# Diagonal score blocks half computed and half mirrored through memory, and a reordered start of the experts

## The chip, the cores and the metric

The kernel runs on one core of one Trainium2 chip. The metric is device time in microseconds (us) of one execution. The median of three runs is 1388.75 us (1388.1 to 1389.97). TensorE multiplies matrices (PE in the profile, with its weight loads as PEld), VectorE is DVE, ScalarE is ACT, GpSimd is POOL, and SyncE (SP) issues most of the DMA transfers, one after the other.

## The reference

For each of 8 batches, with `u`, `v` of 2496 x 256 and `z` of 2496 x 64, all in 32-bit floats:

```python
scores = (1 / S) * z @ z.T
attn   = maximum(scores, 0) ** 2
x      = u * (attn @ v)
```

All 19968 rows of `x` then go to a mixture of 8 experts: a gate `x @ w_gate` picks one expert for each row, each expert keeps the 80 rows with the highest gate weight, and writes `gate * (maximum(x @ w1, 0) @ w2)` for them. Every other row of the output is zero.

## The kernel before

**Tiles.** A batch's 2496 rows are 20 tiles of 128 keys (the last one holds its 64 rows twice, with `v` arranged so that they add up once), taken as 10 pairs. The queries are cut into 5 chunks, `qc` 0 to 4, of 512 columns each; chunk 4 has 448. The main loop has 8 x 5 x 10 = 400 steps `(b, qc, r)`; step `r` handles one pair of key tiles, in the order of `pairs_of[qc]`: 0 to 9, and in chunk 3 first 8 and 9.

**A step.** `scores` runs two steps ahead of its use (LOOK = 2). For each of the pair's two tiles TensorE makes a 128 x 512 block of scores with two matmuls (L326, L327), ScalarE applies Relu (L330) and Square (L331), and the square is split into a rounded high part `ah` and a rest `al` (L105 or L107, and L54). `attend` then adds the pair into two accumulators with twelve matmuls (L358 to L360), the three products of high and low parts for each tile and each half of `v`'s columns.

**Mirrored blocks.** Scores are symmetric. A 512 x 512 block above the diagonal is computed once; VectorE transposes its 32 x 32 squares (L265), SP writes them to memory (`y`, L275) and reads them back with the squares in their mirrored places (`blk`, L292), and `mirrored` only splits the block into `ah` and `al` (L310, L54). SP works through its transfers in program order and waits before the read until the write has landed. Blocks on the diagonal are computed whole: pairs `2*qc` and `2*qc+1`.

**Around it.** While a chunk runs, `finished` treats the chunk before it at fixed steps `r`: `x` is split for the gate, stored transposed (`chunk_store`, L427, and `chunk_store2`), its logits are made, and after a batch the gate's sums and the counts of rows for each expert follow. The next batch's `z` and `v` are loaded and split at fixed steps too. The order on TensorE, ScalarE, VectorE and SP is that of the program text. In the last two chunks of the last batch the first experts' weights are split (`weights_ahead`, L624 and L625).

**After the loop.** The last three key tiles of the last chunk are attended one half of the columns at a time, `x` is formed (`chunk_x_last`, L377), the logits give the last rows' expert (L416 and the operations of `gate_top`), the counts and running sums `incl` give each expert's 80 places, and `ranks` says which running numbers these are.

**The experts** (`ahead`, unit i is expert i). A place is found in three moves: `block` compares its rank with the running sums of blocks of 256 rows, a table row of that block (`wtab`) gives the row inside it, and `token` makes the row number and has GpSimd gather the row of `x` (`xg`, L1104). For units 0 and 1 the table row comes from a TensorE product (`pe_table`, `pe_block`, `pe_fetch`), for the others by a gather from memory (`fetch`, L1046). `whole` reassembles the row, `ffn_x` transposes it, `ffn1` and `ffn2` are the two layers with split weights (L1166, L1196), `result` scales and scatters. `split` rounds one loaded quarter of an expert's weights on ScalarE and takes the rest on VectorE. In this part TensorE, ScalarE, VectorE and GpSimd follow the text, and SP is ordered by the framework.

Of the kernel before, what the change touches and what calls it, by code (L numbers as in the profile page):

```python
# [25 lines left out]
def attn_moe_kernel(ctx, tc, zT, uT, v, wg, w1, w2, out, seq, cap):  # L26
# [172 lines left out]
    def constants():  # L199
        nc.gpsimd.memset(ones_b, 1.0)  # L200
        nc.gpsimd.memset(gall, 0.0)
        for e in range(E):
            nc.gpsimd.memset(first_w[:, :, e:e + 1], float(E - e))
# [24 lines left out]
    tot = const.tile([P, E, NBLK], F32, name="tot")  # L228
    incl = const.tile([P, E, NBLK], F32, name="incl")
    rank = const.tile([P, NST, E], F32, name="rank")  # L230
    ex_last = const.tile([P, NT, E], F32, name="ex_last")
# [14 lines left out]
    pairs_of = [list(range(NP)) for qc in range(NQ)]  # L246
    pairs_of[NQ - 2] = [NP - 2, NP - 1, *range(NP - 2)]
# [9 lines left out]
    to_read = [(b, i, j, (b * NQ + i) * NP + pairs_of[i].index(2 * j) - LOOK)  # L257
# [37 lines left out]

    def pair_tile(tag, b, qc, k, dt=F32R, bufs=3):
        return ew.tile([P, 2, CH], dt, tag=tag, name=f"{tag}_{b}_{qc}_{k}", bufs=bufs)
# [17 lines left out]
    def scores(b, qc, k):  # L315
# [4 lines left out]
        zc, zd = zc_t[b, qc], zd_t[b, qc]  # L320
        a = pair_tile("a", b, qc, k, F32, 2)
        ss = []
        for h in range(2):
            zk = zc_t[b, k // QT][:, (k % QT + h) * P:(k % QT + h + 1) * P]
            s = ps_s.tile([P, CH], F32, tag="s", name=f"s_{b}_{qc}_{k + h}")
            nc.tensor.matmul(s[:, :nq], zk, zc[:, :nq], start=True, stop=False)  # L326
            nc.tensor.matmul(s[:, :nq], zk, zd[:, :nq], start=False, stop=True)  # L327
            ss.append(s)
        for h, s in enumerate(ss):
            nc.scalar.activation(out=a[:, h, :nq], in_=s[:, :nq], func=AF.Relu)  # L330
        nc.scalar.activation(out=a[:, :, :nq], in_=a[:, :, :nq], func=AF.Square)  # L331
        ah = pair_tile("ah", b, qc, k)
        on_v = k // QT == qc or (qc, k) in ON_V and b > 0
        cp(V if on_v else nc.scalar, ah[:, :, :nq], a[:, :, :nq])
        al = pair_tile("al", b, qc, k)
        tt(al[:, :, :nq], a[:, :, :nq], ah[:, :, :nq], ALU.subtract)
# [7 lines left out]
    def attend(b, qc, k, cols=range(DC)):  # L344
        nq = min(CH, seq - qc * CH)
        first, last = 2 * pairs_of[qc][0], 2 * pairs_of[qc][-1] + 1
# [117 lines left out]
    def gate_top(b, q0, q1):  # L464
# [17 lines left out]
        ex = ex_last[:, q0 * QT:q1 * QT] if last else small("ex")  # L482
# [27 lines left out]
    def gate_sum(b, ex, pool):  # L510
# [7 lines left out]
        tt(s4, ex[:, :, 0::2], ex[:, :, 1::2], ALU.add)  # L518
        s2 = small("s2", E // 4)
        tt(s2, s4[:, :, 0::2], s4[:, :, 1::2], ALU.add)  # L520
        s1 = small("s1", 1)
        tt(s1, s2[:, :, 0:1], s2[:, :, 1:2], ALU.add)
        ts(s1, s1, 1e-9, ALU.add)
        V.reciprocal(out=gall[:, col:col + NT], in_=s1.rearrange("p t o -> p (t o)"))
# [8 lines left out]
    def count(k0, k1):  # L533
# [5 lines left out]
        nc.scalar.copy(out=tot[:, :, k0:k1], in_=tp[:, :n].rearrange("p (k e) -> p e k", e=E))  # L539
# [146 lines left out]
    WARM = 3, 6  # L686
    WARM0 = 8
    steps = [(b, qc, r) for b in range(B) for qc in range(NQ) for r in range(NP)]
# [32 lines left out]
    def finished(b, qc, r):  # L721
# [14 lines left out]
        if r == (5 if at_end else 6):  # L736
# [3 lines left out]
        if b < B - 1 and qc == NQ - 1:  # L740
            if r == 7:
                gate_top(b, 0, NQ)
            elif r == 8:
                gate_sum(b, gate_near(b, 0), gp)
        elif qc == 0 and b > 0:
            part = kb - BPB, kb
            if r == 2:
                count(*part)
            elif r == 4:
                up_to(*part)  # L750
                blocks(ps_m, "m", gp, oh, *part)
        elif at_end:
# [12 lines left out]
    with tc.manual_schedule(engines={ET.PE, ET.Activation, ET.DVE, ET.SP}):  # L765
# [11 lines left out]
        for i, (b, qc, r) in enumerate(steps):  # L777
# [4 lines left out]
            if i + LOOK < len(steps):  # L782
                nb, nqc, nr = steps[i + LOOK]
                scores(nb, nqc, 2 * pairs_of[nqc][nr])
# [10 lines left out]
            p = pairs_of[qc][r]  # L795
# [9 lines left out]
            if b + 1 < B:  # L805
                if r == 1:
                    z_raw[b + 1, qc] = load_z(b + 1, qc)
                if r == 5:
                    prep_zc(b + 1, qc, z_raw.pop((b + 1, qc)))
# [3 lines left out]
                if qc == NQ - 1:  # L813
                    g = (r - 1) // 2 if r < 9 else 4
                    if r in (2, 4, 6, 8, 9):
# [12 lines left out]
            mirror_out()  # L828
            if r == NP - 1:
# [183 lines left out]
    def steps_of(own, tl, tw, ps_t, ps_h):  # L1013
        sl, xg_t, tk_t, xs_t, x_t, h_t, hT_t, o_t = {}, {}, {}, {}, {}, {}, {}, {}
# [13 lines left out]

        def block(i):

            st, e = units[i]
            le = tw.tile([P, 1 + NBLK], F32, tag="le", name=f"le_{i}{own}")
            if i < 2:
                nc.gpsimd.memset(le[:, 0:1], 1.0)
# [57 lines left out]
        def token(i):  # L1092
# [16 lines left out]
            tk_t[i] = tok, j, base  # L1109

        def place(i):
# [6 lines left out]
            tk_t[i] = tok, slo  # L1118

        def fetch_gate(i):  # L1120

            ns, (tok, slo) = num(i), tk_t[i]
# [4 lines left out]
            tk_t[i] = gg, slo  # L1127
# [27 lines left out]
        def ffn1(i, part):  # L1155
# [8 lines left out]
            for c in range(DC):  # L1164
                for x, w in ((xh, w1h), (xl, w1h), (xh, w1l)):
                    nc.tensor.matmul(hp[:ns], x[:, c * ns:(c + 1) * ns], w[:, c, f0:f0 + 512],  # L1166
                                     start=n == 0, stop=n == 3 * DC - 1)
                    n += 1
# [242 lines left out]
```

## Time and profile before

| What | Value |
|---|---|
| median of 3 runs | 1388.75 us |
| the profiled execution's own time | 1388.46 us |
| its span, first to last instruction | 1386.6 us |
| TensorE's mean granted clock | 0.992 |
| main loop, first to last attention matmul | about 10 to 1305 us |

The page divides the span into busy time of each engine, and the views used below ask the same trace more closely: a table of stretches, groups of instructions by line, lists of waits, and the timeline. A bracket in a timeline row gives the idle time of the engine just before, and what ended it. The ends of matmuls are modelled, so the distance between two starts says more than a duration.

### The profile page before, as it was taken

To read this page: it belongs to the slowest core of one execution; us is meant where nothing else is said; L and a number is where in the kernel's file an instruction comes from. 1 tells how busy PE (TensorE), PEld (TensorE's weight loads), DVE (VectorE), ACT (ScalarE), POOL (GpSimd) and SP (SyncE) were. 2 spreads that over 40 slices of the span, in tenths; PEclk is the share of its full clock that TensorE was granted. 3 is DMA by queue.
4 is the path that set the end of the run, shared out by engine and by line. 5 is a ranking of instruction groups with operands and counts; after the bars stand their busy time and mean duration, and the time that the engine had idled before them with its cause. 6 is when DMAs were issued, how large, how long until landed. Compare 5 with 4: busy or idle time off the path is not lost. (4 is left out here: it accounts for less than half of the span.)

```text
span 1386.6 us, 19562 instructions
## 1 busy us (share of the span) xinstructions
PE 1367.1 (99%) x7087; PEld 1139.5 (82%) x7087; DVE 1060.6 (76%) x1517; ACT 1008.8 (73%) x1282; POOL 36.5 (3%) x57
## 2 busy tenths in 40 slices
PE   9999999999999999999999999999999999999887
PEld 6888888888888888888888888888888888888666
DVE  8876788668877788767886688777787678867785
ACT  8866687758777587666887577775877668876375
POOL 0000000000000000000000000000000000000062
PEclk9999999999999999999999999999999999999989
DMA  6899877995888958997688958889588986789774
GB/s 223 252 249 271 225 204 239 235 267 143 256 237 231 273 151 245 239 261 197 188 252 232 270 143 259 238 225 274 145 246 239 255 210 179 220 229 252 176 225 141
DMA packets 260070, 311.89 MB, mean 225 GB/s; under 512 B 96152, under 2 KB 188192, under 8 KB 249728
## 3 DMA queue, kind: packets, MB, share of 16 engines
q1 hardware_dynamic: 258752, 309.02, 81.4%
q0 software_dynamic: 1216, 1.56, 0.4%
q8 instruction: 57, 0.93, 0.3%
q14 instruction: 45, 0.37, 0.1%
HBM read 153.48 MB, written 126.37 MB: 202 GB/s over the span
## 5 line engine op out<-in xcount | busy, mean ns | idle before, releaser
L359 PE MATMUL acc<-ah,vt 128*128 128x512 f32 (+1 forms) x1520 | 584.5, 385 | 0.3 <-DVE vt L146 0.3
L360 PE MATMUL acc<-al,vt 128*128 128x512 f32 (+1 forms) x1520 | 584.5, 385 | 0.3 <-DVE al L54 0.2
L358 PE MATMUL acc<-ah,vt 128*128 128x512 f32 (+1 forms) x1520 | 584.2, 384 | 0.0
L54 DVE TENSOR_TENSOR al<-a,ah 128x1024 fp32r<-128x1024 f32 (+1 forms) x240 | 291.5, 1214 | 135.4 <-ACT ah L105 125.6
L330 ACT ACTIVATE a<-s 128x512 f32<-128x512 f32 (+1 forms) x480 | 258.4, 590 | 153.9 <-PE s L327 143.8
L359 PEld LDWEIGHTS acc<-ah,vt 128*128 128x128 f32 x1520 | 285.4, 188 | 53.9 <-DVE vt L146 1.2
L358 PEld LDWEIGHTS acc<-ah,vt 128*128 128x128 f32 x1520 | 285.3, 188 | 52.9
L360 PEld LDWEIGHTS acc<-al,vt 128*128 128x128 f32 x1520 | 285.4, 188 | 52.9 <-DVE al L54 1.2
L331 ACT ACTIVATE a<-a 128x1024 f32<-128x1024 f32 (+1 forms) x240 | 253.0, 1054 | 7.6
L310 ACT CAST ah<-blk 128x1024 fp32r<-128x1024 f32 x160 | 167.0, 1049 | 105.6 <-PE acc L359 88.5
L54 DVE TENSOR_TENSOR al<-blk,ah 128x1024 fp32r<-128x1024 f32 x160 | 193.8, 1216 | 56.1 <-ACT ah L310 53.2
L265 DVE STREAM_TRANSPOSE x<-a 128x512 f32<-128x512 f32 x320 | 207.6, 687 | 0.0
L327 PE MATMUL s<-zd,zc 128*128 128x512 f32 (+1 forms) x480 | 186.5, 388 | 0.0
L105 ACT CAST ah<-a 128x1024 fp32r<-128x1024 f32 x153 | 160.9, 1052 | 4.8
L107 DVE CAST ah<-a 128x1024 fp32r<-128x1024 f32 (+1 forms) x87 | 59.2, 681 | 95.6 <-ACT a L331 95.6
L326 PE MATMUL s<-zc,zc 128*128 128x512 f32 x320 | 128.1, 400 | 0.0
L327 PEld LDWEIGHTS s<-zd,zc 128*128 128x128 f32 x480 | 90.3, 188 | 16.3 <-issue 0.5
L326 PEld LDWEIGHTS s<-zc,zc 128*128 128x128 f32 x320 | 60.1, 188 | 11.1
L326 PE MATMUL s<-zc 128*128 128x512 f32 (+1 forms) x160 | 63.5, 397 | 0.0
L388 ACT CAST xb<-xf 128x1024 bf16<-128x1024 f32 (+1 forms) x39 | 40.0, 1026 | 23.4 <-DVE xf L377 23.1
L396 ACT CAST xb<-xr 128x1024 bf16<-128x1024 f32 (+1 forms) x39 | 39.9, 1024 | 15.5 <-DVE xr L54 15.5
L377 DVE SCALAR_TENSOR_TENSOR xf<-acc,ut 128x512 f32<-128x512 f32 (+2 forms) x82 | 50.1, 653 | 0.0
(171 smaller groups left out, 835.9 us busy)
## 6 DMA issues: line engine op xcount, KB each, us to landing
y<-x SPq DMA_DIRECT2D x80, 1024.0 KB
blk<-y SPq DMA_DIRECT2D x320, 256.0 KB
out<-idle SPq DMA_DIRECT2D x40, 512.0 KB
vraw<-v SPq DMA_DIRECT2D x32, 512.0 KB
ut<-uT SPq DMA_DIRECT2D x32, 512.0 KB
xs<-xq SPq DMA_DIRECT2D x32, 512.0 KB
wraw<-w SPq DMA_DIRECT2D x28, 512.0 KB
zd<-zc SPq DMA_DIRECT2D x78, 128.0 KB
```

What stands on the lines that cost most here:

```text
L54: V.tensor_tensor(out=o, in0=a, in1=b, op=op)
L105: eng.copy(out=o, in_=i)
L107: eng.tensor_copy(out=o, in_=i)
L265: V.transpose(out=x[:, :, :, t].rearrange("p n k s -> p k n s"), in_=a)
L310: nc.scalar.copy(out=natural(ah), in_=src)
L326: nc.tensor.matmul(s[:, :nq], zk, zc[:, :nq], start=True, stop=False)
L327: nc.tensor.matmul(s[:, :nq], zk, zd[:, :nq], start=False, stop=True)
L330: nc.scalar.activation(out=a[:, h, :nq], in_=s[:, :nq], func=AF.Relu)
L331: nc.scalar.activation(out=a[:, :, :nq], in_=a[:, :, :nq], func=AF.Square)
L358: nc.tensor.matmul(o, vt[:, t, 0, cs], ah, start=k == first, stop=False)
L359: nc.tensor.matmul(o, vt[:, t, 1, cs], ah, start=False, stop=False)
L360: nc.tensor.matmul(o, vt[:, t, 0, cs], al, start=False, stop=k == last)
```

## The change

- Diagonal blocks are no longer computed whole, but for three (`whole_block`: the first of all, and the last two chunks of the last batch). The upper pair `2*qc` is computed over all 512 columns (in chunk 4 too) and comes first in the chunk's order; VectorE transposes its right half (`quarter_out`), SP writes 256 KB and reads it back (`quarter_write` at r = 0, `quarter_back` at r = 3, into one buffer). The lower pair `2*qc+1` comes last; its scores are computed from column 256 on, and the left 256 columns are split from the copy in memory.
- To make room, the next batch's `z` and `v` are prepared at other steps, and the finished chunk's store, logits and sums come some steps later.
- The running sums of the last batch's first 18 half tiles are made by one scan after the last attention, instead of eight additions inside the loop; `tot` is kept in 16 bits.
- The last sums of the gate are made by GpSimd, ahead of the experts, and the gate's comparison `gate_near` of the last chunk is put right behind `gate_top`. Three warming matmuls follow the last logits.
- In the experts, units 2 and 3 get their table rows from TensorE too, the rows for units 4 and 5 are gathered before unit 0 begins, the second half of expert 2's weights is loaded at once, `ffn1` does the products of `xl` last, and the weight splits are spread 1, 3, 4, 4, 4, 4, 4 over the units instead of 3, 4, 3, 3, 4, 3, 3, 1.

```diff
+    def whole_block(b, qc):
+        return (b, qc) in ((0, 0), (B - 1, NQ - 2), (B - 1, NQ - 1))
+    def order(b, qc):
+        rest = [p for p in range(NP) if p // 2 != qc]
+        if whole_block(b, qc):
+            return [NP - 2, NP - 1, *range(NP - 2)] if qc == NQ - 2 else list(range(NP))
+        if qc == NQ - 2:
+            rest = rest[-2:] + rest[:-2]
+        return [2 * qc, *rest, 2 * qc + 1]
...
+    def quarter_out(b, qc, a):
+        x = zpool.tile([P, n32, 2, 2, SQ], F32, tag="md", name=f"xd_{b}_{qc}", bufs=1)
+        for t in range(2):
+            V.transpose(out=x[:, :, :, t].rearrange("p n k s -> p k n s"), in_=a[:, t, HQ:])
+        quarter[b, qc] = now[0], x
+    def quarter_write():
+        for (b, qc), (at, x) in list(quarter.items()):
+            if at is not None and at + 2 <= now[0]:
+                y = dram.tile([n32, SQ, n32, 4 * SQ], F32, tag="yd", name=f"yd_{b}_{qc}", bufs=2)
+                nc.sync.dma_start(out=y.rearrange("g p h f -> (g p) (h f)"),
+                                  in_=x.rearrange("p h k t s -> p (h k t s)"))
+                quarter[b, qc] = None, y
+    def quarter_back(b, qc):
+        _, y = quarter.pop((b, qc))
+        m = zpool.tile([P, n32, 2, 2 * SQ], F32, tag="md", name=f"md_{b}_{qc}", bufs=1)
+        for h in range(n32):
+            nc.sync.dma_start(out=m[h * SQ:(h + 1) * SQ].rearrange("p g k f -> p g (k f)"),
+                              in_=y[:, :, h].rearrange("g p f -> p g f"))
+        quarter[b, qc] = None, m
...
+        diag = k // QT == qc and not whole_block(b, qc)
+        lower = diag and k % QT > 0
+        c0, c1 = (HQ, nq) if lower else (0, CH if diag else nq)
...
+            nc.tensor.matmul(s[:, c0:c1], zk, zc[:, c0:c1], start=True, stop=False)
+            nc.tensor.matmul(s[:, c0:c1], zk, zd[:, c0:c1], start=False, stop=True)
...
+        if lower:
+            m = quarter.pop((b, qc))[1].rearrange("p n k (t s) -> p k t n s", t=2)
+            nc.scalar.copy(out=natural(ah), in_=m)
+            tt(natural(al), m, natural(ah), ALU.subtract)
...
+        eng.tensor_tensor(out=s4, in0=ex[:, :, 0::2], in1=ex[:, :, 1::2], op=ALU.add)
+        eng.tensor_tensor(out=s2, in0=s4[:, :, 0::2], in1=s4[:, :, 1::2], op=ALU.add)
+        eng.tensor_tensor(out=s1, in0=s2[:, :, 0:1], in1=s2[:, :, 1:2], op=ALU.add)
+        eng.tensor_scalar(out=s1, in0=s1, scalar1=1e-9, scalar2=None, op0=ALU.add)
...
+        V.tensor_tensor_scan(out=sums.rearrange(fl), data0=keep.rearrange(fl),
+                             data1=pre["count"].rearrange(fl), initial=0.0,
+                             op0=ALU.mult, op1=ALU.add)
+        tt(incl[:, :, k0:k1], sums, incl[:, :, k0 - 1:k0].broadcast_to([P, E, n]), ALU.add)
...
-    SPLITS = dict(zip([(qb, 0), (qb, 2), (qb, 5), (qb, 8), (qz, 2), (qz, 4), (qz, 6), (qz, 8)], early))
+    SPLITS = dict(zip([(qb, 0), (qb, 2), (qb, 5), (qb, 8), (qz, 2), (qz, 4), (qz, 6), (qz, 7)], early))
+    keys_in = {qc: [(qc - 1, 1, 6)] for qc in range(1, NQ)}
+    keys_in[0] = []
+    keys_in[NQ - 1] = [(NQ - 2, 1, 4), (NQ - 1, 4, 7)]
...
-        if r == (3 if at_end else 1):
+        if r == (3 if at_end else 4):
             chunk_store(b, qc)
-        if r == (5 if at_end else 3):
+        if r == (5 if at_end else 6):
             chunk_store2(b, qc)
-        if r == (5 if at_end else 6):
+        if r == (5 if at_end else 6 if qc == NQ - 1 else 7):
             chunk_logits(b, qc)
...
-                count(*part)
-                up_to(*part)
-                half()
+                count(*part, True)
...
+            if b and qc == 0 and r == 3:
+                prep_v(b, NQ - 1, v_raw.pop((b, NQ - 1)), nc.scalar, V)
...
+            quarter_write()
+            if r == 3 and not whole_block(b, qc):
+                quarter_back(b, qc)
...
+        up_to_last((B - 1) * BPB, B * BPB - 2)
+        half()
         chunk_store(*prev)
         chunk_logits_last(*prev)
+        warm(3, ps_s, "s")
         gate_top(b, NQ - 1, NQ)
+        gate_near(b, NQ - 1)
+        gate_rows(b, ex_last, gp, nc.gpsimd)
...
             tot_last(NBLK - 2, NBLK)
+            raw_whole(*RAW[None])
+            pe_fetch(0)
+            warm_up(3)
+            for i in range(2, 4):
+                pe_table(i)
+            within(0)
+            token(0)
+            pe_fetch(1)
+            warm_up(4)
+            within(1)
+            last_gates()
+            token(1)
+            for i in range(2, 4):
+                block(i)
+                pe_block(i)
+            warm_up(2)
+            block(4)
+            fetch(4)
+            whole(0)
+            block(5)
+            fetch(5)
+            ffn_x(0)
+            for i in range(2, 4):
                 pe_fetch(i)
+            ffn_xl(0)
+            within(2)
+            token(2)
             ready.extend(kept)
             loads(2, PL)
             whole(1)
             within(3)
             token(3)
...
```

## Rows read from the trace of the kernel before

**Rows 1.** The page's part 1: busy us (share of span) xinstructions of each engine.

```profile
PE 1367.1 (99%) x7087; PEld 1139.5 (82%) x7087; DVE 1060.6 (76%) x1517; ACT 1008.8 (73%) x1282; POOL 36.5 (3%) x57
```

**Rows 2.** Stretches: busy us of PE, PEld, DVE, ACT, POOL; PEclk, DMA share, GB/s.

```profile
333.90:368.60 34.70, 34.70 (x176) 28.66 (x175) 29.13 (x43) 28.63 (x38) 0.00 (x0) 1.00 0.63 179
368.60:402.90 34.30, 34.30 (x177) 28.07 (x176) 29.22 (x52) 27.44 (x37) 0.00 (x0) 1.00 0.86 248
...
437.60:466.90 29.30, 29.30 (x152) 24.19 (x151) 20.27 (x22) 15.29 (x18) 0.00 (x0) 1.00 0.99 270
...
333.90:495.90 162.00, 162.00 (x837) 136.01 (x836) 124.57 (x168) 119.35 (x150) 0.00 (x0) 1.00 0.84 227
```

**Rows 3.** Timeline of PE in chunks 0 and 4 of batch 2: start us, us, matmul.

```profile
340.22 0.39 PE L326 MATMUL s<-zc,zc 128*128 128x512 f32 x1
...
343.84 0.39 PE L326 MATMUL s<-zc,zc 128*128 128x512 f32 x1
...
471.74 0.36 PE L358 MATMUL acc<-ah,vt 128*128 128x448 f32 x1
...
476.81 0.36 PE L359 MATMUL acc<-ah,vt 128*128 128x448 f32 x1
```

**Rows 4.** Timeline of PE, one unit of the experts: matmuls of 256 columns.

```profile
1336.48 0.80 PE L1181 MATMUL tp<-ident,h 80*128 80x80 f32 x8
...
1340.05 0.28 PE L1196 MATMUL op<-w2h,hTh 128*80 128x256 f32 x1
...
1342.74 0.28 PE L1196 MATMUL op<-w2h,hTl 128*80 128x256 f32 x1
1342.86 0.72 PE L1181 MATMUL tp<-ident,h 80*128 80x80 f32 x8
```

**Rows 5.** Groups by line: xcount | busy us, mean ns of one | idle us before <-releaser.

```profile
L358 PEld LDWEIGHTS acc<-ah,vt 128*128 128x128 f32 x1520 | 285.3, 188 | 52.9
...
L265 DVE STREAM_TRANSPOSE x<-a 128x512 f32<-128x512 f32 x320 | 207.6, 687 | 0.0
...
L54 DVE TENSOR_TENSOR s<-ex_last 128x80 f32<-128x80 f32 x1 | 0.2, 243 | 0.0
```

**Rows 6.** The same view, VectorE alone, from 1300 us to the end.

```profile
L625 DVE TENSOR_TENSOR w2l<-wraw,w2h 128x1024 fp32r<-128x1024 f32 x11 | 13.3, 1223 | 3.8 <-ACT w2h L624 3.7
...
L54 DVE TENSOR_TENSOR hTl<-tp,hTh 128x320 fp32r<-128x320 f32 x16 | 7.1, 483 | 2.0 <-ACT hTh L1185 2.0
L1099 DVE TENSOR_SCALAR_CACHE_REDUCE lw<-wr,rin 80x256 bf16<-80x256 bf16 x6 | 2.8, 470 | 1.1 <-DMA wr<-wtab,idx 1.1
```

**Rows 7.** Waits of SP's queue: waiter <- releaser: us in total, times, longest.

```profile
SPq L292 <- DMA y<-x: 179.5, 38, 8.7
```

**Rows 8.** Timeline of SP and ACT at the start of chunk 2, batch 2.

```profile
393.68 1.76 SPq L292 DMA_DIRECT2D blk<-y  x4
...
402.85 1.05 ACT L310 CAST ah<-blk 128x1024 fp32r<-128x1024 f32 x1 [1.22 <-PE acc L362]
```

**Rows 9.** Timeline behind the main loop, by start.

```profile
1304.63 1.22 DVE L625 TENSOR_TENSOR w2l<-wraw,w2h 128x1024 fp32r<-128x1024 f32 x1
...
1306.24 1.95 PE L416 MATMUL pl<-wg_sb,xf 128*128 128x8 f32 x16 [1.20 <-DVE xf L377]
...
1319.94 0.72 PE L1166 MATMUL hp<-w1h,xTl 128*80 128x512 f32 x1
...
1322.86 0.47 PE L1166 MATMUL hp<-w1h,xTl 128*80 128x512 f32 x1
...
1328.32 0.76 ACT L105 COPY xf<-xg 80x512 uint16<-80x512 uint16 x1 [3.45 <-DMA xg<-xs,tok]
...
1330.84 0.50 PE L1196 MATMUL op<-w2h,hTh 128*80 128x256 f32 x1 [1.35 <-ACT h L1169]
...
1336.27 0.41 PE L1196 MATMUL op<-w2h,hTl 128*80 128x256 f32 x1
```

**Rows 10.** Table of stretches behind the main loop (columns as in rows 2).

```profile
1330.00:1335.00 5.00, 4.02 (x18) 3.64 (x19) 4.93 (x8) 5.00 (x9) 3.49 (x3) 0.50 0.44 149
```

More of the change, by code (lines that the diff above doesn't have):

```diff
@@ L243, in attn_moe_kernel @@
     NP = NT // 2
-    pairs_of = [list(range(NP)) for qc in range(NQ)]
-    pairs_of[NQ - 2] = [NP - 2, NP - 1, *range(NP - 2)]
+    def whole_block(b, qc):
[7 more added lines that the diff above has]
+        return [2 * qc, *rest, 2 * qc + 1]
+    pairs_of = {(b, qc): order(b, qc) for b in range(B) for qc in range(NQ)}
+    HQ = CH // 2
     LOOK, AHEAD = 2, 12
@@ L345, in attend @@
         nq = min(CH, seq - qc * CH)
-        first, last = 2 * pairs_of[qc][0], 2 * pairs_of[qc][-1] + 1
+        first, last = 2 * pairs_of[b, qc][0], 2 * pairs_of[b, qc][-1] + 1
         if k == first:
@@ L481, in gate_top @@
         tt(d, lg, bc(mx), ALU.subtract)
-        ex = ex_last[:, q0 * QT:q1 * QT] if last else small("ex")
+        ex = ex_last[:, q0 * QT:q1 * QT] if last else lg
         nc.scalar.activation(out=ex, in_=d, func=AF.Exp)
@@ L538, in count, with up_to_last @@
                              start=h == 0, stop=h == 1)
-        nc.scalar.copy(out=tot[:, :, k0:k1], in_=tp[:, :n].rearrange("p (k e) -> p e k", e=E))
+        tv = tp[:, :n].rearrange("p (k e) -> p e k", e=E)
+        if last:
+            pre["count"] = gp.tile([P, E, k1 - k0], F32, tag="s4", name="cnt")
+            nc.scalar.copy(out=pre["count"], in_=tv)
+        nc.scalar.copy(out=tot[:, :, k0:k1], in_=tv)
+    def up_to_last(k0, k1):
+        n = k1 - k0
+        fl = "p e k -> p (e k)"
+        sums = gp.tile([P, E, n], F32, tag="fw", name="sums")
+        V.tensor_tensor_scan(out=sums.rearrange(fl), data0=keep.rearrange(fl),
+                             data1=pre["count"].rearrange(fl), initial=0.0,
+                             op0=ALU.mult, op1=ALU.add)
+        tt(incl[:, :, k0:k1], sums, incl[:, :, k0 - 1:k0].broadcast_to([P, E, n]), ALU.add)
     def up_to(k0, k1):
@@ L805, in attn_moe_kernel @@
             if b + 1 < B:
[L806 to L809, printed above, removed]
+                for j, load, prep in keys_in[qc]:
+                    if r == prep:
+                        prep_zc(b + 1, j, z_raw.pop((b + 1, j)))
+                    if r == load:
+                        z_raw[b + 1, j] = load_z(b + 1, j)
                 if qc == NQ - 2 and r in (2, 4):
@@ L1027, in empty, with row @@
             ts(none, none, float(4 * NTOK), ALU.mult)
+        def row(i):
+            return tw.tile([P, 1 + NBLK], F32, tag="le", name=f"le_{i}{own}", bufs=4)
+        if not own:
+            for i in range(4):
+                les[i] = row(i)
+                nc.gpsimd.memset(les[i][:, 0:1], 1.0)
         def block(i):
             st, e = units[i]
-            le = tw.tile([P, 1 + NBLK], F32, tag="le", name=f"le_{i}{own}")
-            if i < 2:
-                nc.gpsimd.memset(le[:, 0:1], 1.0)
+            le = les.pop(i) if i in les else row(i)
             cnt = col("cnt", i)
@@ L1163, in ffn1 @@
             n = 0
[L1164 to L1168, printed above, removed]
+            for ops in (((xh, w1h), (xh, w1l)), ((xl, w1h),)):
+                for c in range(DC):
+                    for x, w in ops:
+                        nc.tensor.matmul(hp[:ns], x[:, c * ns:(c + 1) * ns], w[:, c, f0:f0 + 512],
+                                         start=n == 0, stop=n == 3 * DC - 1)
+                        n += 1
             nc.scalar.activation(out=h_t[i][:ns, f0:f0 + 512], in_=hp[:ns], func=AF.Relu)
@@ L1219, in last_gates @@
         def last_gates():
-            near = tl.tile([P, QT, E], F32, name=f"near{own}")
-            gate_near(B - 1, NQ - 1, near)
             gate_sum(B - 1, ex_last, tl)
@@ L1298, in ahead @@
             tot_last(NBLK - 2, NBLK)
-            for i in range(n_pe):
-                pe_fetch(i)
-                warm_up(WARM[min(i, 1)])
-                within(i)
-                token(i)
-            for i in range(n_pe, min(n_pe + 2, NU)):
-                block(i)
-                fetch(i)
-            last_gates()
-            raw_whole(*RAW[None], PL)
+            raw_whole(*RAW[None])
[21 more added lines that the diff above has]
+            for i in range(2, 4):
+                pe_fetch(i)
+            ffn_xl(0)
+            within(2)
+            token(2)
             ready.extend(kept)
             loads(2, PL)
-            whole(0)
-            ffn_x(0)
             whole(1)
-            within(2)
-            ffn_xl(0)
             within(3)
-            token(2)
             token(3)
-            split(V)
+            for k in range(2):
+                fetch_gate(k)
             for i in range(NU):
@@ L1329, in ahead @@
                     ffn_h(0, 1)
+                    spread(2)
+                    within(4)
+                    take(4)
+                    for k in range(2, 5):
+                        fetch_gate(k)
                     split(V)
@@ L1333, in ahead @@
                     ffn_xl(i + 1)
+                split(V)
+                ffn1(i, 1)
                 if i == 0:
                     empty()
-                    for k in range(n_pe + 2):
+                    for k in range(n_pe):
                         place(k)
-                        fetch_gate(k)
-                    look(4)
-                split(V)
-                ffn1(i, 1)
-                if i == 1 and NU > 2:
+                elif i == 1:
                     ffn_x(2)
                     ffn_xl(2)
-                if i == 0:
-                    spread(2)
-                    look(5)
-                    last_flags(0)
-                else:
+                    look(6)
+                    spread(3)
+                    split(V)
+                else:
+                    if i == 2:
+                        last_flags(0)
+                        within(5)
                     take(i + 3)
```

77 lines of the change are left out of this document (43 added, 34 removed).

## The prediction, made before the changed kernel was run

> **What bounds the kernel now.** I read the page's engine totals first: TensorE is busy 99% of the span, VectorE 76%, ScalarE 73% [rows 1]. Busy is not yet bound, so I cut one batch into its chunks: in each, PE is busy for the whole stretch at clock 1.00, while VectorE and ScalarE have some 5 us of room in 34, and the transfers' share rises to 0.99 in chunk 3 [rows 2]. Then the starts of neighbouring matmuls: 512 columns follow each other every (343.84 - 340.22)/16 = 0.226 us, 448 columns every (476.81 - 471.74)/25 = 0.203 us [rows 3]. A chunk is its matmuls laid end to end: until about 1305 us only a shorter list of matmul columns, or a new hole between two of them, moves the end.
>
> Behind the loop it is otherwise. TensorE waits 1.20 us for `x`, ScalarE 3.45 us for the gathered row of unit 2 and through it TensorE's second layer of unit 0, which then runs at half clock (0.50, the 1.2 GHz level) after that idle stretch [rows 9, 10]. From there on a unit takes 1342.86 - 1336.48 = 6.4 us, matmul behind matmul [rows 4].
>
> **The halved blocks.** Of 40 diagonal blocks 37 change: 30 in chunks 0 to 3 (batch 0: 3, batches 1 to 6: 24, batch 7: 3) and 7 in chunk 4. The lower pair has 2 tiles with 2 score matmuls each. In the 30, these 4 go from 512 to 256 columns. A matmul of 256 columns follows the next in (1342.74 - 1340.05)/23 = 0.117 us in the experts' second layer [rows 4], there with weights of 80 columns. So 4 x (0.226 - 0.117) = 0.436 us per block, 30 of them 13.1 us. In chunk 4 the upper pair grows from 448 to 512 columns, 4 x (0.226 - 0.203) = +0.09 us, and the lower shrinks from 448 to 192. For 192 columns there is no row; below it cannot beat 16 matmuls of 8 columns with 128-column weights, 1.95/16 = 0.12 us [rows 9], above it is at most the 256-column 0.117 unless a weight load decides. I take 0.117 to -0.34 + 0.09 = -0.25, seven of them 1.8 us. Sum -14.9 us.
>
> Both ends: a weight load is shown at 188 ns [rows 5]. If a short matmul cannot start before the next weights are in, a block saves 4 x (0.226 - 0.188) = 0.15 us, 30 blocks 4.6, and chunk 4 nothing: -4.6. The other end is -15.2, a little more from 192 columns. I take -14.9, since the 8-column matmuls with full-width weights come at 0.12 us and not 0.188 [rows 9]. The Trainium skill ("Perfetto Trace Analysis", section Identifying the Most-Contended Engine) speaks against this: it holds matmul busy time to be a bad measure of how near an engine is to its limit and names the busy share of weight loads as a good one. That share is 82% here [rows 1]; by that rule the loads are nearly the bound, and halving columns under the same loads would give the smaller end. The rule's result is rival A.
>
> **What the mirrored quarter adds.** VectorE gets two transposes of 128x256; one of 128x512 takes 687 ns [rows 5], so about 0.7 us, less 0.1 for a shorter cast and rest. ScalarE gives up half of its Relu and Square of the lower pair and gets the cast from memory: about nothing. VectorE's 29.22 us of 34.30 in chunk 1 [rows 2] hold 0.6 us more; chunk 0 has room of 5.6 us on VectorE and 6.1 on ScalarE, into which the last part of the next `v` comes (some 3 us together) while preparation of a `z` leaves. If that cover were gone the bound would be the 0.6 us per block, 22 us over 37 blocks; the upper pair is scored two steps ahead, 7 us, which hides a burst of it. Cost taken: 0, from 0 to +2.
>
> The transfers grow by 0.26 MB out and 0.26 MB back per block. At full share the engines move about 227/0.84 = 270 GB/s [rows 2], so 1.9 us of their time per block. Chunks 0 and 1 have room; chunk 3 does not: 0.99 x 29.3 = 29.0 us of work and 1.9 more in 29.3 - 0.4 us hand 2 us on to chunk 4. SP issues five transfers more per block, and its waits are in order: the quarter's read at r = 3 stands in front of the reads of mirrored blocks. SP now waits 179.5 us in 38 places, 4.7 us each, for a write to land before such a read [rows 7]. A block's read is issued 402.85 - 393.68 = 9.2 us before ScalarE takes it [rows 8]. The quarter is written at r = 0, three steps before its read; a step is 34.3/10 = 3.4 us, so 10 us for the write, and the copy is used four steps, 14 us, after the read. The mirrored pairs also come one step later in the chunk, behind the upper pair, which gives their reads 3.4 us more. Cost taken: 0; what it costs otherwise is rival C.
>
> **Stores, logits and loads at later steps, and the one scan.** In the loop they are the same instructions under the same cover; the chunk before is stored and its logits made up to three steps later, still within the next chunk. Eight additions of the running sums leave VectorE in front of `x`, and a scan and one addition come back behind it, where VectorE waits for the last logits anyway. Zero.
>
> **The start of the experts, part a.** TensorE's 1.20 us wait for `x` is VectorE finishing a weight split at 1304.63 + 1.22 us [rows 9]; with that split one step earlier and the additions gone it goes. `gate_near` now ahead of the counts costs 0.15 us or so. The gate's sums on GpSimd: VectorE's first takes 243 ns [rows 5] and four of that size at most 1.0 us; GpSimd is bounded from this 1.0 us below to twice it above, and stands in GpSimd's order ahead of the memsets that units 0 and 1 compare behind, so 0 to 0.6 us of it shows. The Trainium skill ("GPSIMD Engine Reference", section 3.1, Elementwise) gives an addition of 2048 elements as 4497 ns on GpSimd and 2293 ns on VectorE; no run here shows it, and by it the estimate would be about 2 us, the upper end. Sum of a: -1.0, between -1.2 and 0.
>
> **Part b.** With unit 2's table row made on TensorE, ScalarE's wait of 3.45 us for its gathered row falls away but for some 0.3 us: -3.1. Without the hole the second layer of unit 0 keeps its clock: its 23 intervals took 1336.27 - 1330.84 = 5.43 us against 2.69 at full clock [rows 4, 9]: -2.7. The first layer of unit 0 runs at half clock for 1322.86 - 1319.94 = 2.92 us, seven matmuls that need 1.6 at 0.226: of these 1.3 I take half as saved by the added warming matmuls, -0.6. Against it unit 1's row is reassembled behind the search and row number of unit 2, about 0.47 [rows 6] and some small operations: +0.6. Sum -5.8, between -7.4 and -2.
>
> **Part c.** Four weight splits a unit instead of three on VectorE: 4 x 1.22 = 4.9 us, two `hTl` of 0.48 make 1.0, two searches of 0.47 make 0.9 [rows 6], and the compares, row numbers and flags of about ten operations near 0.2 another 2.2: 9.0 us in unit 2's round against TensorE's 6.4. It becomes late there by 2.6, and in the four rounds behind, without the second search and flags, by about 0.2 each, 0.8. Sum +3.4, between 0 (if splits slide into the last unit, which has none) and +5.
>
> Tail: -1.0 - 5.8 + 3.4 = -3.4, between about -8.5 and +2. With the main loop -18.3 us: the profiled execution, 1388.46 us (0.3 below the median, so either may be compared), becomes 1370.2; I write **1370.0**.
>
> **Rivals.** *A, weight loads hold the short matmuls:* the main loop gives 4.6, the time is 1388.5 - 4.6 - 3.4 = 1380.5. For it: 82% busy loads, 188 ns each; against: matmuls at 0.117 and 0.12 us with loads between them. Chance 0.08.
> *B, the tail gives nothing:* VectorE with four splits a unit takes back part b, tail +1: 1374.5. For it: 9.0 against 6.4 us; against: the hole and the half clock are in the rows. Chance 0.14.
> *C, slower:* SP's wait for the quarter's write delays the reads of mirrored blocks where the transfers are full. If each of the 7 changed chunk 3 lost one mean wait of 4.7 us, 33 us would be lost and 18.3 gained: 1403. It decides from 18.3/37 = 0.5 us lost per changed block on. For it: share 0.99 and reads 9 us ahead only; against: three steps between write and read. Chance 0.04.
> The forecast holds 0.72; 0.02 is left for what I do not see.
>
> **How the numbers follow.** About 0.2% (2.8 us) is what a measurement can tell from no change. The forecast's own ends are 1388.5 - 15.2 - 8.5 = 1364.8 and, with +2 in the loop and a tail of zero, 1375.6; B lies inside. The range 1364 to 1378 goes beyond for losses of 2 us in chunk 3 that add to B, and leaves A, C and a little more out. Faster holds the forecast, A, B and nearly all of the rest (0.94); slower is C; 0.02 is between.
>
> **What the profile after would show.** Score matmuls of 256 columns with starts about 0.117 us apart (right) or 0.188 (A). Batch 2 in 162.0 - 4 x 0.44 - 0.25 = 160.0 us with PE busy throughout; holes in PE behind a cast of the mirrored quarter or of `blk` would be C. The loop's end at about 1290 us. No bracket of 3 us ahead of unit 2's row on ScalarE, and the first `op` matmuls 0.117 us apart; brackets from VectorE's `w1l` or `w2l` ahead of TensorE in units 2 to 6 are part c. The prediction is wrong if the loop's batches shrink by under 1.5 us, or if the end of the loop to the end of the span is longer than now.

## The result, and the profile after

The changed kernel takes 1373.98 us, median of five runs (1373.60 to 1374.92), against 1388.75 us: ratio 0.9895, 95% interval 0.9885 to 0.9906. It is faster by 14.8 us where 18.8 was forecast. The same kernel, run again in two later stays (a stay is one session of runs on one chip), took 1369.88 us (1369.35 to 1370.81; ratio 0.9863, 0.9846 to 0.9879) and 1370.97 us (1369.35 to 1371.39; ratio 0.9865, 0.9849 to 0.9882), with the kernel before at 1389.28 and 1389.25. So the first result of this kernel is 3.0 to 4.1 us above the two later ones, and both have to be explained. E below is the start of the last attention matmul, and the tail is what is left of the span behind E.

| us | before | after | again, 2nd stay | again, 3rd stay |
|---|---|---|---|---|
| span | 1386.6 | 1371.9 | 1367.6 | 1369.6 |
| E | 1304.65 | 1290.63 | 1290.65 | 1291.30 |
| loop: first attention matmul to E | 1294.63 | 1280.59 | 1280.54 | 1280.53 |
| tail | 82.0 | 81.3 | 77.0 | 78.3 |
| E to first second-layer matmul of unit 0 | 26.2 | 20.6 | 20.7 | 20.9 |
| E to that of unit 1 | 35.4 | 26.9 | 27.0 | 27.3 |
| from there to the end of the span | 46.6 | 54.3 | 49.9 | 51.0 |

The loop gave 14.0 to 14.1 us in all three profiles of the changed kernel; in the third stay it only began 0.7 us later. The tail gave 0.7 us in the first stay, 5.0 in the second and 3.7 in the third.

Engine totals after, answering to [rows 1]:

```profile
PE 1352.8 (99%) x7099; PEld 1128.0 (82%) x7100; DVE 1078.2 (79%) x1620; ACT 994.1 (72%) x1322; POOL 37.7 (3%) x62
```

They tell nothing of the gain but its size: PE's busy time fell by 14.3 us, and it is still busy for 99%. The stretches of batch 2 after, with the columns of [rows 2], chunk 3 and the whole batch:

```profile
433.40:462.30 28.90, 28.90 (x152) 23.90 (x150) 21.20 (x27) 16.12 (x21) 0.00 (x0) 1.00 1.06 280
330.00:490.20 160.20, 160.20 (x837) 134.66 (x837) 127.08 (x182) 117.29 (x156) 0.00 (x0) 1.00 0.90 245
```

The batch takes 160.2 us where 160.0 was forecast, chunk 3 is 0.4 us shorter, and PE is busy all through: no new hole, though VectorE does 2.5 us more in the batch and the transfers' share in chunk 3 rises from 0.99 to 1.06. The short score matmuls, timeline of PE after, start first:

```profile
389.02 0.28 PE L370 MATMUL s<-zc 128*128 128x256 f32 x1
389.14 0.28 PE L371 MATMUL s<-zd,zc 128*128 128x256 f32 x1
...
479.41 0.27 PE L371 MATMUL s<-zd,zc 128*128 128x192 f32 x1
479.52 0.27 PE L370 MATMUL s<-zc 128*128 128x192 f32 x1
```

Matmuls of 256 columns follow each other in 0.12 us, those of 192 columns in 0.11, both with weights of 128 columns. That is the forecast's 0.117, and not the 0.188 of a weight load. The forecast set a rule against this (the Trainium skill, "Perfetto Trace Analysis", section Identifying the Most-Contended Engine: the busy share of weight loads, beside the share of the peak rate, tells how near TensorE is to its limit) and worked out 4.6 us for the loop by it. The measured 14.0 decides against that reading here: the loads' rows of 188 ns did not keep the matmuls' starts more than 0.12 us apart.

SP's waits after, for what is read from memory (in total, times, longest), answering to [rows 7]:

```profile
SPq L306 <- DMA y<-x: 73.0, 24, 8.1
SPq L333 <- DMA yd<-xd: 7.1, 2, 3.8
```

L333 reads the quarter back: of 37 such reads 2 waited. SP's waits for a write ahead of a mirrored block fell from 179.5 us to 73.0. Shorter waits would also fit an SP that comes later, so what decides is who waits for the copies. Waits after, of PE and ScalarE, up to the end of the loop:

```profile
PE wp L651 <- ACT tot L606: 1.2, 1, 1.2
PE s L371 <- DVE zd L54: 0.3, 1, 0.3
ACT ah L384 <- DMA md<-yd: 10.5, 10, 1.5
```

ScalarE does wait for the quarter's copy, in 10 of the 37 blocks and for 1.5 us at most, but TensorE waits for nothing that hangs on it: the two lines are all of its waits behind the start of the program.

Behind the loop, timeline after, answering to [rows 9]:

```profile
1290.88 1.93 PE L470 MATMUL pl<-wg_sb,xf 128*128 128x8 f32 x16
...
1294.55 0.32 POOL L572 TENSOR_TENSOR s<-ex_last 128x80 f32<-128x80 f32 x1 [2.43 <-DVE nh L54]
...
1303.88 0.39 PE L1262 MATMUL hp<-w1l,xTh 128*80 128x512 f32 x1
1304.11 0.39 PE L1262 MATMUL hp<-w1h,xTh 128*80 128x512 f32 x1
...
1311.23 0.33 PE L1292 MATMUL op<-w2h,hTh 128*80 128x256 f32 x1
...
1313.98 0.28 PE L1292 MATMUL op<-w2h,hTl 128*80 128x256 f32 x1
```

The logits start 0.25 us behind E with no bracket: the 1.20 us wait is gone. The second layer of unit 0 takes 2.75 us for its 23 intervals where [rows 9] had 5.43: it runs at 2.4 GHz (granted clock 1.00). GpSimd's sums are 0.32, 0.25, 0.22 and 0.28 us, 1.07 in all.

### The profile page after: what moved, and what is told of

The parts are those of the page before. It is cut to its first block, busy times and chain, and to the rows that moved or that the text cites. A ratio compares the mean times of both kernels' runs of the same rounds, so it can differ in the third digit from the quotient of the medians.

```text
span 1371.9 us, 19965 instructions
## 1 busy us (share of the span) xinstructions
PE 1352.8 (99%) x7099; PEld 1128.0 (82%) x7100; DVE 1078.2 (79%) x1620; ACT 994.1 (72%) x1322; POOL 37.7 (3%) x62
## 5 line engine op out<-in xcount | busy, mean ns | idle before, releaser
L54 DVE TENSOR_TENSOR al<-a,ah 128x1024 fp32r<-128x1024 f32 (+1 forms) x240 | 271.8, 1132 | 144.3 <-ACT ah L105 139.6
L374 ACT ACTIVATE a<-s 128x512 f32<-128x512 f32 x480 | 243.3, 559 | 131.1 <-PE s L371 126.5
L375 ACT ACTIVATE a<-a 128x1024 f32<-128x1024 f32 x240 | 237.9, 991 | 7.6
L371 PE MATMUL s<-zd,zc 128*128 128x512 f32 x480 | 177.2, 373 | 0.3 <-DVE zd L54 0.3
L107 DVE CAST ah<-a 128x1024 fp32r<-128x1024 f32 (+3 forms) x87 | 49.0, 563 | 37.9 <-ACT a L375 37.9
L370 PE MATMUL s<-zc 128*128 128x512 f32 (+3 forms) x160 | 55.7, 359 | 0.0
L146 DVE TENSOR_TENSOR vt<-vraw,vt 128x1024 fp32r<-128x1024 f32 (+1 forms) x40 | 46.1, 1152 | 12.2 <-ACT vt L105 12.2
```

The costliest lines, as they stand in the source:

```text
L54: V.tensor_tensor(out=o, in0=a, in1=b, op=op)
L107: eng.tensor_copy(out=o, in_=i)
L370: nc.tensor.matmul(s[:, c0:c1], zk, zc[:, c0:c1], start=True, stop=False)
L371: nc.tensor.matmul(s[:, c0:c1], zk, zd[:, c0:c1], start=False, stop=True)
L374: nc.scalar.activation(out=a[:, h, c0:c1], in_=s[:, c0:c1], func=AF.Relu)
L375: nc.scalar.activation(out=a[:, :, c0:c1], in_=a[:, :, c0:c1], func=AF.Square)
```

## The experiments

Three questions were open: whether the loop's gain is that of the short matmuls alone; what holds the units after unit 1, which now take longer; and what made the first stay 3.0 to 4.1 us slower. In the texts below the theories are named by their mechanism. All medians are of four to six runs, beside the kernel before on the same chip. x1 to x4 are of one stay, x0, x5 and x6 of the second, x8 to x11 of the third, and x12 of a later one.

**x1_whole**: every diagonal block computed whole again, all shifted steps and the new experts kept.

```diff
-        return (b, qc) in ((0, 0), (B - 1, NQ - 2), (B - 1, NQ - 1))
+        return True
```

> The changed kernel, but all diagonal blocks computed whole in the old order of pairs; the shifted steps of stores and loads, the one scan and the new start of the experts stay. Theory 1 (the loop's gain is the shorter score matmuls alone): the end of the loop goes back by the 14.2 us it gained, plus or minus 1; time about 1373.8 + 14.5 = 1388. Rival (the shifted steps and the scan gain a good part by themselves): 1380 to 1385.

1384.49 us (1382.97 to 1388.91), ratio 0.9968 (0.9957 to 0.9980). Timeline of PE, the last attention matmul in x1_whole:

```profile
1304.60 0.37 PE L417 MATMUL acc<-al,vt 128*128 128x448 f32 x1
```

E is where it was before (1304.65), as the first theory has it. The time lies in the rival's range, but that is the tail's doing: it is 78.2 us, near those of the later stays, where the theory counted on the first one's 81.3. The loop, from its first attention matmul on, is 0.2 us shorter than before's, so the stores, logits, loads and the scan at later steps are worth next to nothing, and the rest of the 14.0 us belongs to the halved blocks. Stretches from the first attention matmul of batch 2 to that of batch 3, in x1_whole and then after (columns of [rows 2]):

```profile
333.49:495.46 161.97, 161.97 (x836) 136.03 (x835) 124.97 (x168) 119.25 (x150) 0.00 (x0) 1.00 0.83 227
```

```profile
330.04:490.15 160.11, 160.11 (x836) 134.61 (x835) 127.08 (x182) 117.20 (x156) 0.00 (x0) 1.00 0.90 245
```

The five blocks of a batch are worth 1.86 us.

**x2_blocks_late**: the block totals for the row numbers made once behind the loop, to take away a stall that came up in front of them.

```diff
-            elif r == 9:
-                blocks(ps_m, "m", gp, oh, *part)
...
+        blocks(ps_m, "m", gp, oh, (B - 1) * BPB, B * BPB - 2)
```

> The changed kernel with the last batch's block table (the three matmuls on upper and oh) made behind the last logits instead of at the loop's last step. Theory: in the changed kernel TensorE stands 1.16 us there, behind a weight cast on ScalarE that the change put ahead of the copies of the counts; that stall goes and the table costs about 0.2 us later: 0.8 to 1.1 us faster, 1373.0. Rival: the stall only moves to the next wait for ScalarE or to x: no change.

The stall that this text speaks of, timeline after:

```profile
1285.92 1.03 ACT L700 CAST w2h<-wraw 128x1024 fp32r<-128x1024 f32 x1
...
1286.96 0.21 ACT L606 CAST tot<-tp 128x64 bf16<-128x64 f32 x1
1287.23 0.22 PE L651 MATMUL wp<-upper,oh 128*64 128x128 bf16 x1 [1.16 <-ACT tot L606]
```

The weight split that used to end late in front of `x` now starts one step earlier, and ScalarE's part of it stands ahead of the copy that TensorE waits for: 1.2 us, where the kernel before waited 0.3. In x2 that wait is gone and E is 1290.18, 0.45 earlier; its loop is 1280.04 us, where the other eleven profiles with halved blocks have 1280.4 to 1281.1. The time shows nothing of it, 1373.62 us over a wide 1371.48 to 1377.70 (ratio 0.9890, 0.9877 to 0.9903): its tail was 81.7 us, with a wait of 4.1 us for a scatter at its end. As a way to save 0.5 us it is undecided; that the stall costs some 0.5 us at E is shown.

**x3_split_first, x4_flag_first, x5_both**: VectorE's order in units 2 and 3: one of unit 2's weight splits ahead of its flags; unit 3's flags ahead of its splits; both.

```diff
                     if i == 2:
+                        split(V)
                         last_flags(0)
...
-                    split(*(V,) * 3)
-                if i == 3:
-                    last_flags(1)
+                    if i == 3:
+                        last_flags(1)
+                    split(*(V,) * (2 if i == 2 else 3))
```

> The changed kernel with one of unit 2's three later weight splits put ahead of the flags, the place search of unit 5 and the compares of unit 7. Theory V (VectorE's order in unit 2 starts the loss of the experts' middle, its delay carries on): the 1.3 us stall of TensorE ahead of the second w1l product of unit 3 goes, and with it part of what follows: 1.3 to 4 us faster. Rival S (ScalarE's waits of 1.6, 1.7 and 1.0 us for TensorE there are separate): under 1 us, the waits on ScalarE stay.

> The changed kernel with the last flag (a product on TensorE and one operation on VectorE) ahead of unit 3's three later weight splits, not behind them. Theory: TensorE waits 1.42 us there for the buffer that VectorE's flag releases behind two splits, and runs the next eleven matmuls at half clock; both go: 1.4 to 3 us faster, and the next stretch at full clock. Rival: VectorE is late by the splits themselves, and the next wait is for w1l or hTl: under 0.7 us.

> The changed kernel with both: one of unit 2's later splits ahead of its small operations, and the last flag ahead of unit 3's splits. Theory V (VectorE's order is what is lost in the middle): faster than the unaltered kernel by 1.5 to 4 us. Rival: VectorE's sum of work bounds units 1 to 3 whatever its order: within 1 us.

1370.63 us (1369.57 to 1372.93; ratio 0.9868, 0.9853 to 0.9882), 1369.80 (1369.29 to 1370.17; 0.9858, 0.9844 to 0.9872) and 1370.52 (1369.78 to 1371.05; 0.9866, 0.9849 to 0.9882). Beside 1373.98 they looked like gains; but the unaltered kernel in the same stay as x5 took 1369.88. In the stay of x3 and x4 the unaltered kernel was not run. **x0_after** and **x8_again** are that unaltered kernel:

> The changed kernel once more, unaltered, as the measure for the two beside it and for the tails. In its first profile seven of TensorE's signals to ScalarE between 1320 and 1330 us came 2.6 to 6.1 us after the matmul they tell of; in four altered kernels none did, and one of those with the same experts had a tail of 78.2 us and not 81.3. Theory N (these late signals belong to that stay on the chip, not to the kernel): no late signals, tail 77 to 79 us, 1369.5 to 1371. Rival K (they come with this kernel's own order): late again, 1373.5 to 1375.

> The changed kernel unaltered, a third stay on a chip, and the measure for the three beside it. Theory N (late signals are not the kernel's): as in the second stay, 1369.3 to 1371 and none late; if they come, 1373 to 1375.

So both changes of order together are worth nothing (x5 beside x0_after), x3 and x4 singly show no gain beside the later stays, and comparing across stays misled. A round here is the time from one unit's first second-layer matmul to the next unit's; rounds 1 and 2 are those from unit 1 to unit 2 and on to unit 3. Where the gain went: waits of PE in rounds 1 and 2 of x0_after, then the same in x3, and rounds 1 and 2 of x0_after and round 2 of x4 (columns of [rows 2]):

```profile
PE hp L1262 <- DVE w1l L701: 1.5, 2, 1.3
PE xp L1237 <- DVE flag L749: 1.4, 1, 1.4
PE fp L748 <- DVE hTl L54: 0.2, 1, 0.2
```

```profile
PE fp L748 <- DVE hTl L54: 2.0, 1, 2.0
```

```profile
1317.68:1325.90 8.22, 6.72 (x49) 5.19 (x47) 7.85 (x27) 7.07 (x13) 6.39 (x7) 1.00 0.42 131
1325.90:1334.35 8.45, 6.78 (x47) 5.19 (x47) 7.12 (x14) 6.79 (x12) 6.93 (x6) 1.00 0.90 294
```

```profile
1326.44:1333.54 7.10, 6.58 (x47) 5.27 (x47) 6.09 (x12) 5.81 (x12) 5.88 (x5) 1.00 0.86 298
```

In x0_after all that TensorE waits for in these two rounds, 3.1 us, is VectorE's. x3 does away with the 1.3 us for `w1l`, and TensorE then stands 2.0 us for `hTl`, which VectorE makes behind two splits of the second layer. x4 does away with the 1.4 us flag wait, and round 2 falls from 8.45 to 7.1 us; round 3 then takes 7.4 where it took 6.3. VectorE's backlog is handed on, not removed.

**x6_old_experts**: the new loop and head, with the kernel before's order of the experts (two table rows by TensorE, the others gathered, splits 3, 4, 3, 3, 4, 3, 3, 1).

```diff
-        n_pe = 4
+        n_pe = min(2, NU)
...
-                    split(*(V,) * 3)
+                split(*((V,) if i == 0 else (V, V, V) if i == 4 else (V, V)))
```

> The changed loop, scan, gate sums and ffn1 order, with the experts' order of before: two table rows from TensorE, splits 3, 4, 3, 3, 4, 3, 3, 1. It measures what the new order of the experts is worth by itself. As predicted (parts b and c, -5.8 and +3.4): slower than the unaltered changed kernel by 2.4 us. Rival B (VectorE takes all of it back): equal within 1 us, or faster.

1372.89 us (1371.88 to 1373.72), ratio 0.9883 (0.9866 to 0.9899), 3.0 above x0_after on the same chip; parts b and c together were forecast at 2.4. Stretches of x6 ahead of unit 0's second layer, which starts at 1315.59, and in it:

```profile
1311.00:1315.50 4.50, 1.65 (x8) 0.76 (x6) 2.68 (x13) 2.43 (x5) 3.28 (x5) 1.00 1.08 340
1318.00:1324.00 6.00, 6.00 (x34) 5.08 (x33) 5.89 (x18) 5.11 (x11) 3.05 (x3) 0.75 0.40 118
```

With the old order PE is idle again ahead of unit 0's second layer (1.65 us busy in 4.50), and a granted clock of 0.75 follows. They belong to the order of the experts, and the new order is worth 3 us.

**x9_no_w2l, x10_no_w2h, x11_no_w2, x12_no_load**: which engine holds the middle units. For experts 3 to 7, x9 leaves out VectorE's low part of the second layer's weights, x10 ScalarE's cast to their high part, x11 both, x12 their loads as well. The splits of the first layer's weights, `w1h` and `w1l`, stay in all four.

```diff
+        lean = which == 2 and e > 2 and not late.get("own")
...
-        nc.scalar.copy(out=hv[:, s], in_=rv)
+        if not lean:
+            nc.scalar.copy(out=hv[:, s], in_=rv)
```

(x10's core; x9 has the same condition around the subtraction, x11 returns ahead of both, x12 also loads nothing.)

> Leaves out the low part of the second layer's weights of experts 3 to 7: VectorE's rest is not made, and the products that used it use the high part again, so TensorE's and ScalarE's work stay and VectorE loses two splits of four in units 2 to 6. Theory V (VectorE's sum of work is what the experts' middle pays for): units 1 and 2 come down from 8.2 and 8.5 us to about 6.5, 3 to 4.7 us faster than the unaltered kernel. Rival S (ScalarE's sum, four casts and six smaller ones a unit): under 1 us.

> Leaves out the high part of the same weights: ScalarE's two casts a unit are not made (the first layer's high part stands in), VectorE still takes its four differences. Theory V: under 1 us faster than the unaltered kernel. Rival S: 3 to 4.7 us faster. If both engines are near their limit, each alone gives a part: 1 to 3 us each.

> Leaves out both splits of the same weights, high and low part (the first layer's high part stands in for both). All theories: units 1 to 5 at TensorE's 6.3 to 6.5 us, 4 to 5.5 us faster than the unaltered kernel, 1364.5 to 1366. If it is not, neither engine is the bound of the middle but the order of the small steps is.

> Leaves out both splits of the second layer's weights of experts 3 to 7 and their loads from memory too (10 of the last 20 loads of 512 KB); the first layer's high part stands in. With the splits alone left out, the time stayed, and ScalarE waited 4.8 us in 3 places for the gathered rows xg, whose gathers then took up to 6.0 us from issue to landing beside the weight loads. Theory D (the row gathers wait behind the weight loads, a second limit close behind the splits): they land in about 3 us, ScalarE's wait for xg falls under 1 us, units 1 to 5 at 6.3 to 6.5 us, 1365 to 1367. Rival G (GpSimd's own queue order, each gather behind gate gathers and scatters, sets when rows come): the waits for xg stay, 1369 to 1371.

x9 1373.00 us (1372.23 to 1373.66; ratio 0.9884, 0.9867 to 0.9900), x10 1369.89 (1369.37 to 1370.50; 0.9860, 0.9844 to 0.9877), x11 1370.34 (1369.29 to 1371.05; 0.9864, 0.9848 to 0.9881), beside 1370.97 unaltered. With half of VectorE's splits in units 2 to 6 gone the kernel became slower by 2.0 us, and with neither engine's share of these weights it was no faster than by 0.6. x10's 1.1 us is within the spread of the runs; that ScalarE's casts are the limit (3 to 4.7 us) is out. What TensorE waits for in rounds 1 and 2 of x11:

```profile
PE hp L1268 <- DVE w1l L707: 2.1, 2, 1.3
PE hp L1268 <- ACT w1h L706: 1.1, 1, 1.1
```

The 1.3 us of round 1 are those of x0_after: VectorE makes this `w1l` behind the flags and the place searches, and ahead of the splits that were left out. So in round 1 these runs took away only work that stands behind the instruction TensorE waits for, and the round falls from 8.2 to 7.9 us; x3's order without the second layer's splits would have taken both, and was not run. That VectorE holds round 1 is not refuted. Round 2 is another matter. The flag wait of x0_after is gone, and TensorE waits for `w1h` instead, which ScalarE makes behind its copy of a gathered row, and for the `w1l` taken from it. That copy, for unit 5, on ScalarE's timeline in x0_after, x9 and x11:

```profile
1327.45 0.77 ACT L105 COPY xf<-xg 80x512 uint16<-80x512 uint16 x1 [1.01 <-DMA xg<-xs,tok]
```

```profile
1329.74 0.76 ACT L105 COPY xf<-xg 80x512 uint16<-80x512 uint16 x1 [3.21 <-DMA xg<-xs,tok]
```

```profile
1329.08 0.77 ACT L105 COPY xf<-xg 80x512 uint16<-80x512 uint16 x1 [2.55 <-DMA xg<-xs,tok]
```

GpSimd issues it at 1322.92, 1323.01 and 1323.03 us: from issue to use 4.5 us, 6.7 and 6.1. The stretches from issue to use, in the same order, then round 2 of x11 and of x9:

```profile
1322.92:1327.45 4.53, 4.04 (x25) 3.07 (x26) 4.53 (x7) 2.38 (x6) 3.92 (x3) 1.00 0.69 210
```

```profile
1323.01:1329.74 6.73, 6.41 (x46) 5.02 (x46) 3.35 (x9) 2.37 (x6) 2.86 (x4) 1.00 0.94 307
```

```profile
1323.03:1329.08 6.05, 5.80 (x45) 4.89 (x46) 3.33 (x9) 2.22 (x5) 3.75 (x4) 1.00 0.86 279
```

```profile
1325.63:1334.34 8.71, 6.80 (x48) 5.27 (x48) 4.42 (x10) 4.84 (x10) 4.53 (x5) 1.00 0.91 282
```

```profile
1325.63:1336.91 11.28, 8.80 (x49) 6.32 (x48) 5.30 (x11) 7.17 (x12) 4.89 (x5) 0.77 0.78 255
```

In x11's round 2 VectorE and ScalarE have nearly half of the time free, and it takes 8.7 us all the same. The gather takes longest where the transfers beside it are fullest (share 0.69, 0.86 and 0.94). The likely reason is that splits which are left out or end sooner free the weights' buffers sooner, so the next loads start sooner and lie beside the gather; this is argued from these shares, not shown. In x9 the granted clock falls as well (0.77 in round 2), which the other two avoid. So two limits of about one height follow each other: VectorE's work, and in round 2 the gathers.

x12 should have shown whether the loads delay the gathers. ScalarE's wait for a gathered row is down to one of 1.00 us, but the time is 1372.45 (1372.08 to 1372.85; ratio 0.9884, 0.9867 to 0.9900), above x11's, so the question stays undecided. Its profile has what the first one of the changed kernel has, and this is where the difference between the stays lies. Timeline of PE and ScalarE after:

```profile
1320.38 0.72 PE L1277 MATMUL tp<-ident,h 80*128 80x80 f32 x8
...
1325.72 0.43 ACT L1281 CAST hTh<-tp 128x320 fp32r<-128x320 f32 x1 [1.72 <-PE hp L1262]
...
1326.72 0.16 PE L748 MATMUL fp<-nsb,ones_b 128*128 128x1 bf16 x1 [1.18 <-issue]
...
1327.18 0.43 ACT L1281 CAST hTh<-tp 128x320 fp32r<-128x320 f32 x1 [1.03 <-PE fp L748]
```

The same ScalarE instruction in x0_after, and in x12:

```profile
1322.33 0.74 ACT L1281 CAST hTh<-tp 128x320 fp32r<-128x320 f32 x2
```

```profile
1324.90 0.43 ACT L1289 CAST hTh<-tp 128x320 fp32r<-128x320 f32 x1 [3.10 <-PE xp L1245]
...
1328.44 0.42 ACT L1289 CAST hTh<-tp 128x320 fp32r<-128x320 f32 x1 [3.12 <-remote]
```

TensorE's second layer of unit 1 and the transposes behind it are at the same time in after and x0_after (0.12 us apart). In x0_after ScalarE takes the transposed rows at 1322.33 us, with no wait; in after it is free from 1321.96 and waits, and takes them at 1325.72 and 1327.18, 4 to 6 us behind the matmuls' modelled ends. From there the delay runs on: `hTl` is late, PE idle for 1.18 us, and the granted clock is 0.77 from 1332 to 1338 us. Rounds 1 and 2 take 9.2 and 11.6 us instead of 8.2 and 8.45: 4.1 us of the 4.3 between the two spans. It stands in 2 of the 13 profiles of the changed kernel and its variants, and not in that of before. One of the two leaves out half of the last weight loads, so these cannot be the whole cause; and x12 ran on the chip of x8 to x11, none of which shows it, so the chip alone does not decide it either. Whether TensorE's signal came late or ScalarE was late to act on it the rows cannot tell. The cause was not found, and stays open.

## Why the prediction was right

**The halved blocks**: forecast 14.9 us, measured 14.0. The intervals came nearly as worked out (0.12 against 0.117), and x1_whole shows that the rest of the change adds only 0.2 us in the loop. The difference is in the price of a block: a batch gives 1.86 us between x1_whole and after where 4 x 0.436 + 0.25 = 2.0 was forecast. The term set to zero, "stores, logits and loads at later steps", came out near zero as a sum of two: the weight split moved ahead of `tot` made a wait of 1.2 us where 0.3 was, worth some 0.5 us at E by x2, and batch 0, 0.5 us shorter in x1_whole than before, gave it back. For 192 columns the forecast's lower bound of 0.12 us was no bound: 0.11 was measured.

**The quarter's cost of zero**: right. ScalarE waits 10.5 us for the copies in the whole loop and PE not at all, and VectorE's 2.5 us more in the batch stay in its room. Rival C is out: chunk 3 became 0.4 us shorter and TensorE has no new hole, though the transfers there are full.

**Parts a and b**: forecast 6.8 us up to unit 1's second layer, measured 8.4. The wait for `x`, the hole and the half clock of unit 0's second layer are gone as said. Too small was the term for its first layer: it runs 0.23 us apart from its second matmul on, and the forecast took only half of that gain, 0.6 of 1.3. The other 0.9 us are not traced to a term. GpSimd's sums, put at 1 to 2 us, took 1.07; its addition of 128x80 takes 0.32 us where VectorE's took 0.24 [rows 5]. The forecast had them ahead of the memsets that units 0 and 1 need; they run at 1294.55 to 1295.87, 2.4 us behind those, and TensorE has no wait for them.

**Part c**: forecast a loss of 3.4 us from unit 1's second layer to the end, measured 3.4 in the second stay and 4.5 in the third. Size and engine were right, the spread over the rounds was not. The loss is 1.9 us in round 1 and 1.3 in round 2 (8.2 and 8.45 us, against 6.35 and 7.1 before), not 2.6 in one round with 0.2 in each of four behind; a later round loses 0.7 and the end gives 0.5 back. TensorE's waits in rounds 1 and 2, 3.1 us where before had 0.6, are all for VectorE. What the forecast did not see is the limit next to it: with VectorE's second-layer splits taken away (x9, x11), round 2 is held by the gathered row and nothing is gained.

**The total**: 1370.0 was forecast; 1369.88 and 1370.97 in two stays, 1373.98 in the first. That two of them lie so near is partly luck: the loop gave 0.9 us less and parts a and b 1.6 us more than forecast. The forecast's ends for the tail were added up a little off as well (-8.6 and +3 by its own terms, not -8.5 and +2), which changes nothing here. The first result is near rival B's 1374.5, but not by its mechanism: there the tail gave 0.7 us because ScalarE took TensorE's results late between 1320 and 1330 us, which no row of before could show. With the old order x6 loses 3.0 us, so the order does give something, and rival B is out; A is out by the matmuls at 0.12 us.

## What to carry to other kernels

Where one engine is busy throughout a stage, price a change there by the distance between the starts of like instructions, and look up a row of the very shape, however small its group: here it forecast 14.9 us where 14.0 came. Before work is taken from an engine to test whether it is the limit, look which instruction of it the waiting engine waits for, and whether the work taken away stands ahead of that instruction: in x9 to x11 it stood behind. And where a second limit is near, here a gather, taking work from the first buys nothing. Run the unaltered kernel again in the same stay as every variant: without x0_after, x4 would have passed for a gain of 4 us.

## What the runs showed of the hardware

- Matmuls of 256 and of 192 columns with 128-column weights start 0.12 and 0.11 us apart, under weight loads whose rows show 188 ns.
- A gather of 80 rows took 4.5 us from issue to use while the transfers' share beside it was 0.69 (x0_after), 6.1 us at 0.86 (x11) and 6.7 us at 0.94 (x9).
- In two of the 13 profiles ScalarE, free and by the profile waiting only for TensorE, took up its results 4 to 7 us after the matmuls' modelled ends; in the others it has other work until then or follows at once.
